# A gated-linear-attention and Mamba kernel: eleven warming matmuls of 64 columns in place of three of 256

## The chip, the cores and the metric

The kernel runs on one core of a Trainium2 chip. The time is the device time of one execution in microseconds, as the median of several runs; lower is better. A profiled execution has a time of its own and a span, the stretch from the first to the last record of its trace.

## The reference

Two blocks follow one another, all in fp32. The first is a recurrent attention with a gate alpha for every step and channel (B = 4, H = 8, S = 768, D = 48); the second takes its output as x (4 x 768 x 384) through a gated Mamba-like layer with an inner width of 512.

```python
for t in range(S):                                   # attention
    state = alpha[:, :, t, :, None] * state + einsum('bhd,bhe->bhde', k[:, :, t], v[:, :, t])
    y[:, :, t] = einsum('bhd,bhde->bhe', q[:, :, t], state)
x = y.transpose(0, 2, 1, 3).reshape(B, S, H * D)
val, gate = split(x @ w_in)                          # 384 x 1024
a = exp(A_log)
for t in range(S):                                   # one decay, a[0, 0], for all channels
    h = a[0, 0] * h + val[:, t, :]
    ys[:, t, :] = h
out = (silu(gate) * ys) @ w_out                      # 512 x 384
```

## The kernel before

The work is cut into twelve groups of 256 steps (three to a batch). In a group the alphas of 128 step-rows are brought into a layout with channels on partitions, scanned into cumulative products (`scan_P`, L635, and their inverse form `scan_V`, L654, on VectorE), and q and k are scaled by them. TensorE then makes the scores of the group's chunks (`scores`, L798), the values inside a chunk (`first_values`, L918, in the first group, `values`, L834, later), the states (`states`, L866) and what is carried from chunk to chunk (`first_carried`, L926, and `carried`, L847). `project` multiplies x by w_in (L988), scans h on VectorE (L995), applies the gate (L1006, L1008), and `output` multiplies by w_out (L1064).

The order of all instructions is written out by hand: the program is one long straight list per engine (a manual schedule), so an instruction's place in its engine's program is the order of the calls in the source. There are no loops left on the chip. At the end a flag is read and the program branches: in the usual case into a short block that makes the last outputs (twelve passes at L1377).

The head of the program, in order:

- Loads. `load_steps` (L422) brings alphas, q and k of the first groups on the queues of SP and ACT; `load_w` (L454) brings pieces of w_in as raw bits (`wbits`), two DMAs of 384 KB for each of the four pieces. On SP's queue at the head: alphas, q, k, alphas and k of the second group, the first two `wbits`, then q of the second group.
- `constants()` on GpSimd and others, which makes the identity `ident`.
- `keep_warm(3, 256)`: matmuls of a constant zero block by constant zeros, into the PSUM bank y0, which nothing reads before it is written anew. It depends on no load.
- `first_alphas` (L716 to L743): 64 turns of 64 x 64 on TensorE at L723, as soon as the first alphas have landed, and their copies out of PSUM. "Turn" means a matmul with the identity that transposes a tile.
- `first_q` (L745): turns of the first q at L750 and L759. `straighten(0, "k")`: turns of the first k at L702 and L703, and then those of the second alphas (`alphas(1)`) at the same lines.
- `scan_P(0)`, `scan_V(0)`, scaling, `scores(0)` (L798), with turns of the second k in two halves (`turned`, L702 and L703) ahead of and behind it.
- The first piece of w_in is put together from its bits (`low`, `high`, `add_low`, L543 to L556), then the second `load_w` is issued on SP, behind a one-element memset of its tile on VectorE (L1143).
- `first_values` (L918), `states(0)` (L866), a first half of the turns of the second q; then SP issues the alphas of the third group, the third `load_w`, and further loads.
- `first_carried` (L926), `first_values` again, the second half of the turns of the second q (L707), `first_join`, and from then on the projections (L988) with the work of the next groups between them.

Every fp32 matmul of a real product is two passes in the records: each pass has a weight load (LDWEIGHTS, engine PEld) and a MATMUL (engine PE).

Of the kernel before, what the change touches and what calls it, by code (L numbers as in the profile page):

```python
# [346 lines left out]
def fast(  # L347
# [339 lines left out]
    def bank(tag=None):  # L687
        if tag:
            return ps_at.tile([C, 512], FP32, tag=tag, name=tag)
        return ps_mm.tile([C, 512], FP32, tag=f"mm{next(taken)}", name="mm")  # L690
# [25 lines left out]
    def first_alphas():  # L716
        raw, to = steps_of("a", 0), by_runs(by_place(als[0])[:, :, 1:GP])
        tps = [[bank(tag)[:, 0:NJ // 2 * 64].rearrange("p (j x) -> p j x", x=64) for tag in tags]
               for tags in (("s0", "s1"), ("y1", "y0"))]

        def turn_quarter(j, i, r):
            rows = ds(64 * r, 64)
            nc.tensor.matmul(tps[j // 4][r][ds(64 * i, 64), j % 4], raw[rows, ds(i * ROW + j * D, 64)],  # L723
                             ident[rows, rows], start=True, stop=True, skip_group_check=True)

        for j in range(2):
            for r in range(2):
                turn_quarter(j, 1, r)
        for j in range(NJ):
            for r in range(2):  # L730
                turn_quarter(j, 0, r)
                if j + 2 < NJ:
                    turn_quarter(j + 2, 1, 1 - r)
        copies = []
        for n in range(2):
            for r in range(2):
                place = to[:, :, ds(16 * r, 16), 4 * n:4 * n + 4]
                part = tps[n][r].rearrange("p j (c h) -> p h c j", h=4)
                copy = nc.vector.tensor_copy(out=place, in_=part) if r else \
                    nc.scalar.activation(place, part, AF.Copy)  # L740
                for other in copies[1 - r::2]:
                    tc.declare_no_dep(copy.ins, other.ins, reason="the copies write different steps")
                copies.append(copy)  # L743
# [32 lines left out]
    def keep_warm(n, w):  # L776
        t = bank("y0")
        for _ in range(n):
            nc.tensor.matmul(t[:, 0:w], nc.const_aps.tensor(0.0, [C, C], FP32),
                             nc.const_aps.tensor(0.0, [C, w], FP32), start=True, stop=True,  # L780
                             skip_group_check=True)
# [334 lines left out]
        for _ in range(count):  # L1116
            next(steps, None)

    keep_warm(3, 256)
    first_alphas()  # L1120
    for t in sums:
        nc.scalar.activation(t[:, :, D:64], wide_S[0][:, 0:4 * (64 - D)].rearrange("p (j d) -> p j d", j=4), AF.Copy)
# [234 lines left out]
@with_exitstack  # L1357
def kernel(ctx: ExitStack, tc: tile.TileContext, *args):
    nc = tc.nc
    out = args[-1]  # L1360
    C, GC, NI = 128, 256, 4
    B, S, DM = out.shape
    keep = ctx.enter_context(tc.tile_pool(name="keep", bufs=1))
    ps_mm = ctx.enter_context(tc.tile_pool(name="ps_mm", bufs=1, space=bass.MemoryType.PSUM))
    w_outs = [keep.tile([C, 2, DM], FP32, name=f"w_out{i}") for i in range(2)]
    f_last = keep.tile([C, NI, GC], FP32, name="f_last")
    rows = ctx.enter_context(tc.tile_pool(name="rows", bufs=3))
    with tc.manual_schedule():
        good = fast(tc, *args, w_outs, f_last, ps_mm, rows)
    with tc.If(good <= 0, preferred_fallthrough_block=True, label="last") as choice:  # L1370
        general(tc, *args, w_outs)
    with choice.Else(), tc.manual_schedule():
        half = DM // 2
        for i, c, at, size in ((0, 0, 0, DM), (1, 1, 0, half), (3, 1, half, half)):
            o = ps_mm.tile([C, 512], FP32, tag=f"mm{i}", name="mm")[:, 0:size]
            for cc in range(NI):
                nc.tensor.matmul(o, f_last[:, cc, ds(c * C, C)], w_outs[cc // 2][:, cc % 2, ds(at, size)],  # L1377
                                 start=(cc == 0), stop=(cc == NI - 1))
            if not at:
                o_sb = rows.tile([C, DM], FP32, tag="o_sb", name="o_sb")  # L1380
            if c and not at:
                nc.vector.tensor_copy(out=o_sb[:, 0:half], in_=o)
            else:
                nc.scalar.activation(o_sb[:, ds(at, size)], o, AF.Copy)
            nc.scalar.dma_start(out=out[B - 1, ds(S - GC + c * C, C), ds(at, size)], in_=o_sb[:, ds(at, size)])
# [30 lines left out]
```

## Time and profile before

| | |
|---|---|
| median of 3 runs | 270.24 us |
| lowest and highest | 270.16, 270.4 us |
| the profiled execution, its own time | 270.68 us |
| its span | 269.0 us |
| busy of TensorE, VectorE, GpSimd, ScalarE | 98%, 87%, 61%, 41% of the span |
| granted TensorE clock | 1.0 |

Times in rows are in microseconds from the start of the span. In a timeline a row is a run of like instructions of one engine: start, duration up to the last result, engine, line, operation, tiles, shapes and count, and in brackets the idle time ahead of it with what ended it. In a row of windows the stretch comes first, then its length, and for each engine the busy time with the count of instructions that started in it; behind POOL stand the granted clock, the busy share of the 16 DMA engines and GB/s. A group row ends in busy time, mean duration of one in ns, and idle time before. In the list of DMA queues a row is the queue and kind, packets, MB, and the share of the time of 16 engines in the stretch asked for. A row of DMA issues ends in the size and the microseconds from issue to landing. "issue" as the cause of idle time means that the engine waited for nothing that the profile shows.

### The profile page before, as it was taken

How to read it: one execution, taken by the hardware profiler on the slowest of the kernel's cores; microseconds unless marked ns; L12 is line 12 of the kernel's file. 1: busy time of each engine (PE TensorE's matmuls, PEld its weight loads, DVE VectorE, ACT ScalarE, POOL GpSimd, SP SyncE). 2: the span in 40 equal slices, each digit the busy share in tenths (PEclk: the TensorE clock that was granted, in tenths of full speed). 3: DMA queues.
4: the chain of work that ended last, by engine and by line, in shares of the span. 5: the costliest groups of instructions: out<-in, count | busy, mean ns of one | idle time of the engine just before them, and what ended most of it. 6: DMA issues, size and time to landing. Idle time of an engine off the chain costs nothing.

```text
span 269.0 us, 9976 instructions
## 1 busy us (share of the span) xinstructions
PE 263.0 (98%) x4168; PEld 230.2 (86%) x4168; DVE 233.5 (87%) x316; ACT 111.6 (41%) x270; POOL 165.3 (61%) x185
## 2 busy tenths in 40 slices
PE   7989999999999999999999999999999999999995
PEld 5978889886688988988988988988988989988974
DVE  7978898996999999999999999999999998883440
ACT  4666776281242631632543533524524515314011
POOL 8222304093267998996985995996886987646000
PEclk9999999999999999999999999999999999999999
DMA  5938974796993659559687478569588501201201
GB/s 173 316 117 281 296 172 139 210 225 159 243 220 90 138 159 231 119 140 229 133 227 170 107 207 184 113 173 219 128 210 172 144 3 29 75 3 37 70 7 59
DMA packets 52304, 41.19 MB, mean 153 GB/s; under 512 B 27392, under 2 KB 50944, under 8 KB 52256
## 3 DMA queue, kind: packets, MB, share of 16 engines
q1 hardware_dynamic: 49328, 37.34, 56.1%
q0 software_dynamic: 1536, 2.20, 3.1%
q10 hardware_dynamic: 1392, 0.99, 1.3%
q8 instruction: 34, 0.56, 0.9%
q14 instruction: 14, 0.11, 0.1%
HBM read 32.54 MB, written 4.72 MB: 139 GB/s over the span
## 4 chain that ended last, share of the span: by engine, by line
PE 96%; DMA 2%; issue 0%; ACTq 0%; ACT 0%
PE mm L988 48%; PE mm L1064 16%; PE y L834 4%; PE y L847 4%; PE mm L1022 4%; PE s L798 4%; PE mm L798 3%; PE s L866 3%; PE mm L707 2%; PE mm L1377 2%; DMA raw_q<-in_q_dram 2%; PE mm L702 2%; PE mm L703 1%; PE y L918 1%; PE mm L750 1%; PE y L926 1%
## 5 line engine op out<-in xcount | busy, mean ns | idle before, releaser
L988 PE MATMUL mm<-xT,w_in 128*128 128x256 f32 x576 | 129.4, 382 | 0.0
L988 PEld LDWEIGHTS mm<-xT,w_in 128*128 128x128 f32 x576 | 107.9, 190 | 16.0 <-issue 0.5
L1006 ACT ACTIVATE sg<-mm 128x256 f32<-128x256 f32 x48 | 18.4, 383 | 88.9 <-PE mm L988 88.9
L1008 POOL TENSOR_TENSOR f_last<-sg,hh 128x256 f32<-128x256 f32 x36 | 28.8, 806 | 26.1 <-ACT sg L1006 22.6
L886 POOL TENSOR_TENSOR sum<-sum,dS 128x192 f32<-128x192 f32 x30 | 39.3, 1310 | 3.0 <-ACT dS L874 1.4
L635 DVE TENSOR_TENSOR_SCAN P<-al,lower 128x1028 f32<-128x1028 f32 x12 | 30.5, 2541 | 0.3
L995 DVE TENSOR_TENSOR_SCAN hh<-a_dec,hh,mm 128x256 f32<-128x256 f32 x32 | 23.3, 728 | 8.4 <-PE mm L988 8.2
L654 DVE TENSOR_TENSOR_SCAN V<-al,ends 128x1028 f32<-128x1028 f32 x12 | 28.5, 2375 | 0.4
L963 POOL DMA_DIRECT2D xT<-yst x44 | 22.6, 518 | 5.4 <-ACT yst L960 4.0
L556 POOL TENSOR_TENSOR w_in<-w_in,wr 128x768 int32<-128x768 int32 x4 | 7.3, 1820 | 26.3 <-DVE wbits L1143 9.3
L1064 PE MATMUL mm<-wide,wr 128*128 128x192 f32 x108 | 20.8, 327 | 0.0
L600 DVE STREAM_TRANSPOSE k<-raw_k 128x1024 f32<-128x1024 f32 x9 | 18.5, 2053 | 0.0
L600 DVE STREAM_TRANSPOSE q<-raw_q 128x1024 f32<-128x1024 f32 x9 | 18.2, 2026 | 0.0
L1064 PEld LDWEIGHTS mm<-wide,wr 128*128 128x128 f32 x108 | 18.0, 190 | 0.0
L874 ACT ACTIVATE dS<-s 128x384 f32<-128x384 f32 (+1 forms) x18 | 7.4, 461 | 24.4 <-PE s L866 24.4
L818 POOL TENSOR_TENSOR AK<-AK,mask 128x512 f32<-128x512 f32 x9 | 13.7, 1520 | 5.9 <-ACT AK L814 5.7
L600 DVE STREAM_TRANSPOSE al<-raw_a 128x1024 f32<-128x1024 f32 x8 | 16.4, 2045 | 0.0
L619 DVE TENSOR_TENSOR Zk<-k,V 128x1024 f32<-128x1024 f32 (+1 forms) x14 | 15.8, 1128 | 0.1
L1064 PE MATMUL mm<-w_out,f_last 128*128 128x192 f32 x72 | 15.6, 339 | 0.0
L610 DVE TENSOR_TENSOR Zq<-q,P 128x1024 f32<-128x1024 f32 (+1 forms) x14 | 15.2, 1083 | 0.0
L847 PEld LDWEIGHTS y<-Zq,sum 48*64 48x64 f32 x656 | 11.6, 134 | 3.5 <-issue 3.0
L834 PE MATMUL y<-AK,v 64*64 64x64 f32 x352 | 14.5, 221 | 0.0
(188 smaller groups left out, 503.7 us busy)
## 6 DMA issues: line engine op xcount, KB each, us to landing
v<-in_v_dram SPq DMA_DIRECT2D x22, 192.0 KB, 3.6
out_dram<-o_sb SPq DMA_DIRECT2D x22, 192.0 KB, 2.7
raw_k<-in_k_dram SPq DMA_DIRECT2D x18, 184.0 KB, 4.6
raw_q<-in_q_dram SPq DMA_DIRECT2D x18, 184.0 KB, 4.7
raw_k<-in_k_dram SPq DMA_DIRECT2D x18, 176.0 KB, 4.9
raw_q<-in_q_dram SPq DMA_DIRECT2D x18, 176.0 KB, 4.7
wbits<-in_moe_w_in_dram SPq DMA_DIRECT2D x8, 384.0 KB, 5.7
raw_a<-in_alpha_dram SPq DMA_DIRECT2D x16, 184.0 KB, 3.6
```

The costliest lines, as they stand in the source:

```text
L600: nc.vector.transpose(out=by_runs(to).rearrange("p h c j -> p h j c"), in_=raws[name][:, 0:4 * ROW].rearrange("p (h j d) -> p h j d", h=4, ...
L635: nc.vector.tensor_tensor_scan(out=P, data0=al[:, 0:4 * GP], data1=lower.rearrange("p h t -> p (h t)"), initial=0.0, op0=ALU.mult, op1=ALU ...
L654: nc.vector.tensor_tensor_scan(out=V[:, ::-1], data0=al[:, 1:4 * GP + 1][:, ::-1], data1=ends.rearrange("p h t -> p (h t)")[:, ::-1], init ...
L798: nc.tensor.matmul(scs[m][c][i][ds(L * h, L), ds(p * (L + D), L + D)], Zk[rows, c, p, ds(h * L, L)], Zq[rows, u, p], start=True, stop=True ...
L834: nc.tensor.matmul(ys[m][i][ds(64 * s, 64), e, ds(c * C + h * L, L)], v_sb[rows, c, 4 * i + p, :], As[i][rows, c, p, :], start=across and ...
L847: nc.tensor.matmul(ys[m][i][ds(64 * s, 64), e, ds(u * L, L)], Ss[j][rows, p, :], Zqs[m % 2][rows, u, p, D:], start=False, stop=True, skip_ ...
L886: nc.gpsimd.tensor_add(Ss[j][:, :, 0:D], Ss[j - 1][:, :, 0:D], part)
L963: engines[n % len(engines)].dma_start(out=xT[to, a], in_=st[rows, i, e])
L988: nc.tensor.matmul((pv, pg)[vg], w_ins[cc][:, kk, vg, :], xT[:, kk, :], start=(kk == 0), stop=(kk == NK - 1))
L995: nc.vector.tensor_tensor_scan(out=hh, data0=a_dec[:, cc:cc + 1].to_broadcast([C, GC]), data1=pv, initial=prev_h[cc][:, GC - 1:GC] if n % ...
L1008: f = lambda: engine.tensor_mul(fs[n][cc], sg, hh)
L1064: nc.tensor.matmul(o, a[:, k], b[k] if type(b) is list else b[:, k], start=start and k == 0, stop=k == KC - 1, skip_group_check=True)
```

## The change

The warming matmuls at the head become eleven of 64 columns instead of three of 256. They stand in the same place, write the same bank and read the same constants. All else in the source is the same; on the other engines the instructions and their order are the same too. On TensorE, 22 passes stand ahead of the first turn where there were six.

```diff
-    keep_warm(3, 256)
+    keep_warm(11, 64)
     first_alphas()
```

with, unchanged,

```python
def keep_warm(n, w):
    t = bank("y0")
    for _ in range(n):
        nc.tensor.matmul(t[:, 0:w], nc.const_aps.tensor(0.0, [C, C], FP32),
                         nc.const_aps.tensor(0.0, [C, w], FP32), start=True, stop=True,
                         skip_group_check=True)
```

## The prediction

> **What bounds the kernel now.** I read the page first: busy shares, then the chain that ended last.
>
> ```profile
> PE 263.0 (98%) x4168; PEld 230.2 (86%) x4168; DVE 233.5 (87%) x316; ACT 111.6 (41%) x270; POOL 165.3 (61%) x185
> q8 instruction: 34, 0.56, 0.9%
> PE 96%; DMA 2%; issue 0%; ACTq 0%; ACT 0%
> L988 PE MATMUL mm<-xT,w_in 128*128 128x256 f32 x576 | 129.4, 382 | 0.0
> ```
>
> TensorE is busy 98% of the span and is 96% of the chain, so a delay or gain of TensorE that no later wait absorbs is carried to the end. The waits of PE over the whole span say where it is ever late:
>
> ```profile
> PE y L779 <- PEq L1400: 1.0, 1, 1.0
> PE y L926 <- issue: 0.8, 1, 0.8
> PE mm L750 <- DMA raw_q<-in_q_dram: 0.7, 1, 0.7
> ```
>
> Only three: the start, the first turned q at 6.29 us, and 0.8 us at L926 for which no semaphore is named ("issue"). The timeline of PE and PEld, with the group row of the six loads, shows the places:
>
> ```profile
> 1.00 2.92 PE L779 MATMUL y<-const-float32-0.0 128*128 128x256 f32 x6 [1.00 <-PEq L1400]
> 0.99 2.21 PEld L779 LDWEIGHTS y<-const-float32-0.0 128*128 128x128 f32 x6 [0.99 <-issue]
> L779 PEld LDWEIGHTS y<-const-float32-0.0 128*128 128x128 f32 x6 | 1.8, 328 | 1.3 <-issue 1.0
> 4.03 0.88 PE L723 MATMUL s<-ident,raw_a 64*64 64x64 f32 x25
> 6.29 1.96 PE L750 MATMUL mm<-ident,raw_q 128*64 128x128 f32 x24 [0.71 <-DMA raw_q<-in_q_dram]
> 8.18 0.63 PE L759 MATMUL mm<-ident,raw_q 128*64 128x128 f32 x4
> 18.86 0.46 PE L926 MATMUL y<-Zq,wide_S 48*64 48x64 f32 x16
> 20.16 0.39 PE L926 MATMUL y<-Zq,wide_S 48*64 48x64 f32 x7 [0.84 <-issue]
> 22.40 1.09 PE L707 MATMUL mm<-ident,raw_q 128*64 128x128 f32 x16
> 23.43 1.78 PE L988 MATMUL mm<-xT,w_in 128*128 128x256 f32 x7
> 25.40 0.73 PEld L988 LDWEIGHTS mm<-xT,w_in 128*128 128x128 f32 x4 [0.38 <-ACT a_dec L1167]
> ```
>
> L926 stops in the middle of 23 like passes, after its sixteenth, and goes on 0.84 us after the last result: not a missing operand, I read, but missing program. The page's q8 row holds 34 instruction packets with 0.56 MB, 16 KB each, for 2 x 4168 passes and loads, so one packet holds about 245 to 256 instructions, some 125 passes. Counts of passes up to each break (windows from the start) agree:
>
> ```profile
> 0.00:8.15 8.15, 6.32 (x94) 5.00 (x94) 6.46 (x23) 3.24 (x11) 6.87 (x16) 1.00 0.68 202
> 0.00:16.10 16.10, 14.27 (x219) 12.36 (x220) 13.47 (x34) 9.04 (x24) 6.87 (x16) 1.00 0.74 221
> 0.00:20.10 20.10, 17.49 (x346) 15.23 (x347) 16.51 (x40) 11.49 (x28) 8.70 (x17) 1.00 0.66 201
> 0.00:25.30 25.30, 22.63 (x474) 19.69 (x474) 21.50 (x46) 14.29 (x35) 8.70 (x17) 1.00 0.70 214
> ```
>
> PE's breaks at L926 (pass 346) and at L988's load (pass 474, where the load is 0.38 late) are 128 passes apart; 127 earlier lies pass 219, a small hitch at 16.1. So the program's blocks begin at passes 94, 219, 346 and 474. The DMA view of four narrow windows holds one q8 packet each: 13.7 to 15.0, 17.3 to 18.7, 22.8 to 23.9 us (in this order; the first had none between 4 and 13.5):
>
> ```profile
> q8 instruction: 1, 0.02, 5.5%
> q8 instruction: 1, 0.02, 5.8%
> q8 instruction: 1, 0.02, 5.0%
> ```
>
> Shares are of 16 engines: 0.055 x 16 x 1.3 = 1.14 us, 1.30 us and 0.88 us, so each nearly fills its window and the starts are 13.8, 17.35 and 22.9 us. The passes that each releases start at 16.1, 20.16 and 25.40: a block is usable 2.3 to 2.8 us after its fetch starts. After pass 474 PE has no gap in the waits above.
>
> **The change part by part.** *Count and columns.* Three fp32 matmuls are six passes (x6), so eleven are 22: 16 passes, 32 instructions, more. Columns fall from 6 x 256 to 22 x 64 per pass, 1536 to 1408. Six passes of 256 took 2.92 us to the last result, 0.43 us a step (2.92 less a tail of some 0.35, by six), 1.67 ns a column: 64 columns would stream in 0.107 us. The weight load of each is still 128 columns, and no row shows a load longer than its stream. Bounds for a step: 0.107 us (load wholly hidden; 22 steps, end near 3.6 us) and, from the 328 ns of one load record, which holds some latency too, an estimate of 0.21 us, the double (end near 5.7 us). The first turn waits until 4.03, by its PEld on the arrival of raw_a; the next DMA wait of PE ends at 6.29 with 0.71 us of idle. I take 0.107 to 0.17 us, end 3.6 to 4.9, because the six loads from 0.99 to 3.20 never delayed their streams. Cost: nothing; the cover is those 0.71 us. If the step is 0.21, the turns start 1.7 us late, PE's own idle absorbs 0.7, and what the Vector work behind the turns loses could cost up to 0.7.
>
> *The shift.* Every block boundary now falls 16 passes earlier in the code: old passes 78, 203, 330, 458 in place of 94, 219, 346, 474. Their times in the trace:
>
> ```profile
> 0.00:7.00 7.00, 5.17 (x78) 3.99 (x80) 5.31 (x23) 3.17 (x10) 5.78 (x15) 1.00 0.62 179
> 0.00:14.86 14.86, 13.03 (x202) 11.32 (x202) 12.57 (x31) 7.89 (x20) 6.87 (x16) 1.00 0.79 238
> 0.00:18.85 18.85, 17.02 (x330) 14.86 (x330) 15.26 (x39) 10.81 (x26) 8.38 (x17) 1.00 0.66 199
> 0.00:22.85 22.85, 20.18 (x458) 17.85 (x460) 19.16 (x43) 11.89 (x30) 8.70 (x17) 1.00 0.69 208
> ```
>
> Block by block, with the loads that share the DMA engines (issue rows of SP, and landing times of single issues at 7.73, 17.63 and 20.26 us):
>
> ```profile
> 6.84 1.26 SPq L454 DMA_DIRECT2D wbits<-in_moe_w_in_dram  x2
> 8.15 1.36 SPq L422 DMA_DIRECT2D raw_q<-in_q_dram  x2
> 17.21 1.80 SPq L454 DMA_DIRECT2D wbits<-in_moe_w_in_dram  x2
> 19.67 1.19 SPq L422 DMA_DIRECT2D raw_a<-in_alpha_dram  x2
> wbits<-in_moe_w_in_dram SPq DMA_DIRECT2D x1, 384.0 KB, 8.2
> wbits<-in_moe_w_in_dram SPq DMA_DIRECT2D x1, 384.0 KB, 4.5
> raw_a<-in_alpha_dram SPq DMA_DIRECT2D x1, 192.0 KB, 5.1
> ```
>
> A fetch is asked for, as I read it, when PE enters the block before: 8.15 for the one that starts at 13.8, 16.1 for 17.35 (1.2 us, with little else to move), 20.16 for 22.9, where the two wbits loads and the first raw_a were queued ahead.
>
> First block, needed at 14.86 instead of 16.1: asked for at 7.0 instead of 8.15, so between the two wbits issues and no longer behind both. It needs to start by 12.4; the second wbits lands at 7.73 + 8.2 = 15.9, its fetch went 2.1 us ahead of that, and with only one of the two ahead it should be 2 to 3 us earlier, 10.8 to 11.8. Expected stall 0, and the hitch at 16.1 (0.1) goes.
>
> Second block, needed at 18.86: asked for at 14.86, start up to 14.9 + 1.2 = 16.1, or 16.4 if the raw_q loads of 8.15 hold it; usable at 18.4 to 19.2. Stall 0 to 0.3 in place of 0.84 at L926: PE runs 0.7 to 1.0 us ahead of before from there, 0.95 by the value that I take, no stall and the hitch of 16.1 gone too.
>
> Third block, needed now at pass 458, in the L707 turns. Without the old stalls PE would be there near 21.9 (22.85 less 0.95). It is asked for near 18.9 and ready to start by 20.1 at the latest: behind the wbits issue of 17.63 that takes 4.5 us to land (22.1), and before or among the raw_a packets. By the first block's relation the fetch goes 1.1 to 2.1 us ahead of that landing: 20.0 to 21.0. I take 21.0, the late end, since the third fetch of before also went only at 22.9, after all of it. Usable at 23.3 to 23.8: a stall of 1.4 to 1.9 in the L707 turns. From pass 458 to 474 lie half of the sixteen L707 passes, 0.55 us, and eight of L988 at 129.4 / 576 = 0.225, 1.80: 2.35 us. Pass 474 started at 25.40 before. With the middle of 2.3 to 2.8, and a little for the restart, 2.65 from start to use, it starts later by (start + 2.65 + 2.35) - 25.4 = start - 20.4. For 21.0: **+0.6 us**, and 0 at 20.4. Bounds: -0.4 (20.0) to +1.0 (21.4).
>
> Later blocks had no stall; a pass takes 263.0 / 4168 = 0.063 us in the mean, so 125 of them 7.9 us, against some 4 us (1.2 + 2.7) that a fetch needs. Blocks of short passes lie between, so I cost the shift there at nothing, at most 0.3 us. At the end the program branches and fetches its last blocks:
>
> ```profile
> 260.28 3.39 PE L1377 MATMUL mm<-w_out,f_last 128*128 128x384 f32 x12
> ```
>
> L988 passes run up to 260.28 without a gap and hide the branch; the boundary there moves onto the first L1377 load, whose fetch starts some 2.7 us ahead of use: 0, with +2.7 if it were asked for only at the branch.
>
> Sum on the profiled execution: 270.68 + 0.6 = 271.3. It lies 0.44 above the median of 270.24, so the median goes to 270.8.
>
> **The rivals.** *1, the other side: the third fetch does not wait for the wbits queue.* If it starts as soon as asked for, 18.9 to 20.1, PE keeps most of the 1 us: start - 20.4 = -1.5 to -0.3, -1.0 at 19.4. POOL's add of the next w_in limits it to some -1.1, since it runs to 27.15 and L988 needs it near 28.4:
>
> ```profile
> 25.34 1.81 POOL L556 TENSOR_TENSOR w_in<-w_in,wr 128x768 int32<-128x768 int32 x1 [6.17 <-ACT q L714]
> ```
>
> It gives 270.24 - 1.0 = 269.2. It decides where the start is before 20.4. For it: the second fetch started after 1.2 us; against it: the first and third took 5.6 and 2.7 us under queued loads. [...]
>
> *2: the fetch comes later than reckoned.* If the first fetch still waits for both wbits loads it starts at 13.8 again, is usable at 16.1 and costs 1.3 at pass 203; the later two then start when they did, 17.35 and 22.9, with 16 passes more behind them: 22.9 - 20.4 = +2.5. If instead the third waits behind the first raw_a, about 21.6 to 22.9, it is +1.2 to +2.5. Together 271.4 to 272.7, middle 272.1.
>
> *3: nothing moves.* If the gap at L926 isn't missing program, 16 passes ahead of a covered wait change nothing: 270.2. [...]
>
> [...]
>
> **How the numbers follow.** Forecast (third fetch behind wbits, +0.6) 0.42; rival 1 0.29; rival 2 0.16; rival 3 0.06; rival 4 0.07. A measurement of this kernel can tell 0.2%, 0.54 us. Faster by more: nearly all of rival 1 and the lowest of the forecast, 0.29. Within: 0.16 of the forecast's 0.42 (its -0.4 to +0.5), rival 3, a little of the rest, 0.23. Slower: 0.48. The time is 270.8; the forecast's own range is 269.9 to 271.3. The range for 8 in 10 reaches to rival 1's limit, 269.1, and to the middle of rival 2 with some more, 272.3.
>
> **What would show it.** Right: 22 L779 passes ending by about 4.0; L926 at 18.9 without a gap; a gap "issue" of 1.4 to 1.9 us inside L707 near 22 us, before any L988; one q8 packet starting about 21.0; the last L988 of the project that starts at 23.43 later by 0.6. Rival 1: that packet before 20 and no gap over 0.5 at L707. Rival 2: a gap at 14.9, or the packet after 21.6. Wrong altogether: the gap still after sixteen L926 passes, or first turns later than 4.5 us.

## The result and the profile after

The change is slower: 273.6 us (273.13 to 273.83, four runs) against 270.2 (269.88 to 270.4, four runs), a ratio of 1.013 with a 95% interval of 1.0114 to 1.0146, or +3.4 us. The forecast was 270.8, its range ended at 272.3. The profiled execution after took 273.83 us with a span of 272.1.

The page of after: TensorE is still the bound, and busy for 3.9 us more.

```profile
PE 266.9 (98%) x4184; PEld 235.1 (86%) x4184; DVE 233.8 (86%) x316; ACT 111.7 (41%) x270; POOL 164.9 (61%) x185
PE 98%; issue 0%; ACT 0%
```

Its waits of PE, the rows that answer to the three shown of before:

```profile
PE y L779 <- PEq L1400: 1.0, 1, 1.0
PE mm L707 <- issue: 0.9, 1, 0.9
```

The gap in L926 is gone, one in L707 has come, and the wait for the first q is gone because PE now comes later than q. The timeline of PE after, at the head and around that gap:

```profile
1.00 4.94 PE L779 MATMUL y<-const-float32-0.0 128*128 128x64 f32 x22 [1.00 <-PEq L1400]
5.87 1.19 PE L723 MATMUL s<-ident,raw_a 64*64 64x64 f32 x30
8.05 3.35 PE L750 MATMUL mm<-ident,raw_q 128*64 128x128 f32 x24
11.33 0.63 PE L759 MATMUL mm<-ident,raw_q 128*64 128x128 f32 x4
21.79 0.62 PE L926 MATMUL y<-Zq,wide_S 48*64 48x64 f32 x22
24.27 0.66 PE L707 MATMUL mm<-ident,raw_q 128*64 128x128 f32 x8
25.79 0.66 PE L707 MATMUL mm<-ident,raw_q 128*64 128x128 f32 x8 [0.86 <-issue]
26.38 2.86 PE L988 MATMUL mm<-xT,w_in 128*128 128x256 f32 x12
```

Three things are to be read here. The 22 warm passes end at 5.94, so a step is about 0.21 us (4.94 less the tail of the last, by 22; from the second pass on their starts are 213 ns apart), and the first turn starts at 5.87 instead of 4.03. The 24 passes of L750 take 3.35 us instead of 1.96: they run at half speed, with starts 213 ns apart (8.32, 8.53, 8.74) where those of before are 109 apart (6.45, 6.56, 6.67). Up to 10.6 us a pass lasts 426 ns in the mean, in before 277; the turns at L702 that follow last 273 in both. In before the turns of L723 go from 366 ns to 217 by 4.31. I call this speeding up the rise of the clock: near 10.9 us after, near 4.3 before, and the low clock is the stretch ahead of it. (The column of granted clock shows 1.0 over both stretches, as the first two rows below have it; the slow start is seen only in the durations.) So L759 starts at 11.33 instead of 8.18, 3.15 us late. And L707 breaks after eight of its sixteen passes, which is old pass 458, the boundary that the shift by 16 puts there: in the third row below, 474 passes have started ahead of the break, 458 and the 16 added.

```profile
8.00:10.80 2.80, 2.80 (x23) 2.75 (x22) 2.54 (x2) 1.27 (x7) 0.07 (x1) 1.00 0.99 297
10.80:14.00 3.20, 3.20 (x31) 3.03 (x29) 2.67 (x3) 2.06 (x4) 0.00 (x0) 1.00 0.96 299
0.00:25.75 25.75, 23.93 (x474) 22.53 (x475) 19.11 (x43) 12.63 (x33) 8.67 (x17) 1.00 0.60 188
```

Against the first trace of before, PE is 3.15 us late behind L750, 2.9 at the first L926, 1.9 behind its sixteenth pass (the old gap is saved), 2.9 behind the new gap in L707, and 3.16 at the last L1377.

### The profile page after: what moved, and what is told of

The parts are those of the page before. It is cut to its first block, busy times and chain, and to the rows that moved or that the text cites. A ratio compares the mean times of both kernels' runs of the same rounds, so it can differ in the third digit from the quotient of the medians.

```text
span 272.1 us, 10008 instructions
## 1 busy us (share of the span) xinstructions
PE 266.9 (98%) x4184; PEld 235.1 (86%) x4184; DVE 233.8 (86%) x316; ACT 111.7 (41%) x270; POOL 164.9 (61%) x185
## 4 chain that ended last, share of the span: by engine, by line
PE 98%; issue 0%; ACT 0%
PE mm L988 47%; PE mm L1064 16%; PE y L834 4%; PE y L847 4%; PE mm L1022 4%; PE s L798 4%; PE mm L798 3%; PE s L866 3%; PE mm L707 2%; PE mm L1377 2%; PE y L779 2%; PE mm L702 2%; PE mm L703 1%; PE mm L750 1%; PE y L918 1%; PE y L926 1%
## 5 line engine op out<-in xcount | busy, mean ns | idle before, releaser
L988 PE MATMUL mm<-xT,w_in 128*128 128x256 f32 x576 | 129.2, 382 | 0.0
L988 PEld LDWEIGHTS mm<-xT,w_in 128*128 128x128 f32 x576 | 108.0, 190 | 15.6 <-issue 0.5
L995 DVE TENSOR_TENSOR_SCAN hh<-a_dec,hh,mm 128x256 f32<-128x256 f32 x32 | 23.3, 728 | 8.3 <-PE mm L988 8.1
L834 PE MATMUL y<-A,v 64*64 64x64 f32 x352 | 14.7, 221 | 0.0
```

Source lines behind the costliest of these rows:

```text
L834: nc.tensor.matmul(ys[m][i][ds(64 * s, 64), e, ds(c * C + h * L, L)], v_sb[rows, c, 4 * i + p, :], As[i][rows, c, p, :], start=across and ...
L988: nc.tensor.matmul((pv, pg)[vg], w_ins[cc][:, kk, vg, :], xT[:, kk, :], start=(kk == 0), stop=(kk == NK - 1))
L995: nc.vector.tensor_tensor_scan(out=hh, data0=a_dec[:, cc:cc + 1].to_broadcast([C, GC]), data1=pv, initial=prev_h[cc][:, GC - 1:GC] if n % ...
```

## The experiments

In all of them but e11 and e12, which run the change and before as they are, `keep_warm` was given one or two more arguments, the weight columns `p` and, where needed, the bank `t`; nothing that the outputs depend on is left out in any of them. A "short" matmul is one weight column by one streamed column: two passes of program in about 0.06 us (the 16 short passes of e5 begin at 5.98 and L750 follows them at 6.45, about 29 ns a pass). Differences are of medians, in us, against runs of before on the same chip; before spread from 269.4 to 272.1 over these chips in nearly all of its runs, so under 0.3% only intervals count.

**The shift alone, at the head** (e1).

```diff
     keep_warm(3, 256)
+    keep_warm(8, 1, 1)
```

> The three warming matmuls of 256 columns stay, and eight more of one weight column and one streamed column follow them: 16 passes of program more, almost no time. Theory A (the 3.4 us come from the time of the warm passes and a later rise of the clock; the shift of the program only moves a gap): first turn near 4.0 us, turns as short as before, no gap inside L926, a gap of 0.8 to 1.9 us in L707; time 269.9 to 270.9. Theory B (the shift of the program is what costs): 272.5 or more, with PE late behind new gaps.

Measured 272.03, ratio 1.005 (1.0028 to 1.0073), times from 270.72 to 273.43. It misses Theory A's number and stays under B's. The profile tells why it is no clean test: the short passes made the first turn 0.4 us late, and the clock rose near 10.3 us, behind all of L750 (3.67 us for its 24 passes, 1.96 in before). Timeline of PE:

```profile
6.62 3.67 PE L750 MATMUL mm<-ident,raw_q 128*64 128x128 f32 x24
24.75 0.66 PE L707 MATMUL mm<-ident,raw_q 128*64 128x128 f32 x8 [0.82 <-issue]
```

**Shorter weight loads** (e2, and once more as e15), the change with 64 weight columns:

```diff
-    keep_warm(3, 256)
+    keep_warm(11, 64, 64)
```

> Eleven matmuls of 64 streamed columns, but with 64 weight columns instead of 128; 22 passes as in the change. Theory A1 (a load and its stream add up in these passes, 107 and 107 ns): steps of 160 ns, last warm result near 4.8 us, first turn near 4.7; time 270.5 to 273. Theory A2 (the load alone sets the step at 213 ns, hidden stream): steps of 107 ns, warm end near 3.6, clock up near 4.3, time as with the shift alone, 269.9 to 270.9. Theory B (shift): 272.5 or more with either step.

Measured 271.71, ratio 1.0055 (1.0036 to 1.0075). Timeline of PE of e2:

```profile
1.00 2.60 PE L779 MATMUL y<-const-float32-0.0 128*64 128x64 f32 x22 [1.00 <-PEq L1400]
3.90 1.16 PE L723 MATMUL s<-ident,raw_a 64*64 64x64 f32 x26 [0.30 <-DMA raw_a<-in_alpha_dram]
6.26 1.96 PE L750 MATMUL mm<-ident,raw_q 128*64 128x128 f32 x24 [0.28 <-DMA raw_q<-in_q_dram]
22.64 0.66 PE L707 MATMUL mm<-ident,raw_q 128*64 128x128 f32 x8 [0.56 <-issue]
```

As many passes, as much streamed, half the weight columns: 22 passes in 2.60 us, steps of 0.107, turns on time, L750 at full speed. The step is Theory A2's: it halves with the weight columns, 213 ns with 128 and 107 with 64, so the load sets it. The gap in L707 stays. The profiled execution took 270.40, but the median is 1.35 over before; A's number is missed again.

**Less to stream per load** (e4) and **fewer passes of 64 columns** (e3):

```diff
-    keep_warm(3, 256)
+    keep_warm(11, 16)      # e4
+    keep_warm(3, 64)       # e3
```

> Eleven matmuls of 16 streamed columns with 128 weight columns. Theory A1 (load and stream add): steps of about 134 ns, warm end near 4.1 us. Theory A2 (the load alone is 213 ns): steps of 213 ns as with 64 columns, first turn near 5.9. Either way the streams are sparse, and the clock should rise late; time 271.5 to 273.6.

> Three matmuls of 64 columns: program as long as before, warm passes end near 2.5 us, so the first turn is not late. Theory A (a clock that rises only after dense streaming): turns and L750 at half speed, first rise later than 7 us, time 271.0 to 272.5. Theory B (shift alone costs): as before, 270.2, within 0.5.

e4 took 274.29 (one run, above the 273.6 expected), e3 271.27, ratio 1.0029 (1.0012 to 1.0045). The rows of e4, then of e3:

```profile
1.00 4.87 PE L779 MATMUL y<-const-float32-0.0 128*128 128x16 f32 x22 [1.00 <-PEq L1400]
```

```profile
1.00 1.53 PE L779 MATMUL y<-const-float32-0.0 128*128 128x64 f32 x6 [1.00 <-PEq L1400]
6.21 3.58 PE L750 MATMUL mm<-ident,raw_q 128*64 128x128 f32 x24
```

A quarter of the columns, the same 0.21 us a step (4.87 us for 22 passes, 4.94 in the change): A2 again, what is streamed adds nothing to the step of 213 ns. In e3, with the program as long as before and no turn late, the poor warming alone keeps L750 at half speed (rise near 9.5 us) and costs 0.9.

**The shift alone, behind the first turns** (e5), **and lateness with and without it** (e7, e8).

```diff
     keep_warm(3, 256)
     first_alphas()
     ...
+    spare_bank = ps_mm.tile([C, 512], FP32, tag="mm3", name="mm")
+    keep_warm(3, 512, C, spare_bank)         # e7, e8 only; there keep_warm(3, 256) goes
+    keep_warm(8, 1, 1, spare_bank)           # e5, e8 only
     tq = first_q()
```

> The three warming matmuls of 256 columns stay; the eight with one weight and one streamed column now come behind the first turns, into the wait for the first q. So every block boundary from the second on lies 16 passes earlier, and the head is as before. Theory C (the shift moves the gap from L926 to L707 and is worth -0.4 us when PE is on time, as in the trace with 64 weight columns): no gap in L926, 0.6 to 0.9 us in L707, 269.8 to 270.4 against before. Theory D (the shift costs by itself, since the later gap is not covered by a late head): 0.8 to 1.5 us over before.

> No warm pass ahead of the first turns; three matmuls of 512 columns (six passes, so no shift) stand between the turns and L750, which makes PE about 3 us late at L750. Theory C (the gap in L926 takes up lateness when the blocks lie as before): PE 2.5 to 4 us late at L759, the gap in L926 gone, 1.2 to 2 us late at pass 474 and so 271.4 to 272.3. Theory D' (lateness of the head is carried whole): 273 or more.

> As the one before, with the eight short matmuls behind the 512-column ones: late by the same, and the boundaries 16 passes earlier. Theory C: the gap in L707 comes whatever the lateness, so it is 0.8 to 1.4 us slower than the one before. Theory D': the same as the one before within 0.5.

e5: 271.1, ratio 1.0046 (1.0028 to 1.0063), +1.1: Theory D. e7: 273.03, 1.0111 (1.0082 to 1.0141), +3.0, with L750 at 9.88, 3.6 late against 6.29: Theory D', the lateness is carried. It is not carried quite whole: against the profile of before it falls from 3.6 at L759 to 2.3 at the end of the span, since e7 has no gap in L926, and against that of e12 below from 4.1 to 3.1. e8: 275.16, 1.0181 (1.0149 to 1.0212), with L750 at 10.73: 0.85 later than in e7, and 2.1 slower, so some 1.3 is the shift's. That misses D' (the same as e7 within 0.5) and fits the part of Theory C by which the gap in L707 comes whatever the lateness. The other part, a gap at L926 that belongs to the kernel and brings the time of e7 down to 272.3, fell. The rows of e5, and of e8, at the gap:

```profile
23.07 0.66 PE L707 MATMUL mm<-ident,raw_q 128*64 128x128 f32 x8 [0.83 <-issue]
```

```profile
27.08 0.66 PE L707 MATMUL mm<-ident,raw_q 128*64 128x128 f32 x8 [0.86 <-issue]
```

**Before once more** (e12) showed where Theory C was wrong.

> The kernel before once more, for a second profile. [...] Theory F': at 4.3 again.

269.81 us (one run). The clock rose near 4.4, close to the 4.3 of Theory F'. L926 and L707 in its timeline, and then all its waits of PE:

```profile
18.87 0.62 PE L926 MATMUL y<-Zq,wide_S 48*64 48x64 f32 x22
21.35 1.09 PE L707 MATMUL mm<-ident,raw_q 128*64 128x128 f32 x16
```

```profile
PE y L779 <- PEq L1400: 1.0, 1, 1.0
PE s L723 <- DMA raw_a<-in_alpha_dram: 0.3, 1, 0.3
PE s L798 <- DVE Zq L610: 0.3, 1, 0.3
PE mm L798 <- ACT k L714: 0.2, 1, 0.2
```

There is no gap for missing program at all. Its DMA view has a q8 packet in the window from 8.8 to 10.1 us:

```profile
q8 instruction: 1, 0.02, 4.6%
```

The first fetch started near 9 us here, at 13.8 in the trace that the prediction used. The gap in L926 that I took for the kernel's own stands in one of two profiles of before. A late first fetch goes with it there, but does not make it alone: e3 and e7, unshifted too, have their first packet at 12.7 and 14.0 us and no gap in L926, with PE itself 1.3 and 3.4 us later there. Measured against the trace of e12, the shift costs 0.7 us in e2 and 1.0 in e15, the two profiles with 64 weight columns: the start of the ninth L707 pass, 22.64 and 22.75 against 21.84, less the lateness just ahead of it, 0.1 and -0.1.

**Smaller shifts** (e9 four short matmuls, e10 two, at e5's place).

> As the shift behind the first turns, with four short matmuls instead of eight: boundaries 8 passes earlier, at old passes 86, 211, 338 and 466. Theory C: the first block is still fetched early, the gap at L926 is gone, and the one at pass 466 is 0.5 us shorter than at 458, so 0.4 to 0.9 us faster than before in an execution whose clock rises by 6 us; lateness of the head is carried on where the clock rises later. Theory D (the shift costs by itself): as with 16 passes or slower, 0.5 to 1.5 us over before.

> Two short matmuls, 4 passes, boundaries at 90, 215, 342 and 470. Theory C: if the first fetch is early enough (start by 12 us), no gap over 0.3 us anywhere and 0.8 to 1.2 us faster; if it still starts behind the queued wbits loads near 13.8, the gap in L926 is there as before, and the time is that of before within 0.5.

e9: 270.5, ratio 1.0015 (0.9997 to 1.0034); e10: 270.44, 1.0011 (0.9994 to 1.0027). Neither can be told from before. The rows: e9's gap, at pass 466, the first of L988, as the boundaries say, and e10's waits of PE, with none for program.

```profile
22.83 2.86 PE L988 MATMUL mm<-xT,w_in 128*128 128x256 f32 x12 [0.37 <-issue]
```

```profile
PE y L779 <- PEq L1402: 1.0, 1, 1.0
PE s L723 <- DMA raw_a<-in_alpha_dram: 0.3, 1, 0.3
```

So the gap moves with the boundary and shrinks as more of the longer L707 and L988 passes come ahead of it: 0.83 at 458 (e5), 0.37 at 466, none at 470, or at 474 in e12. The gain that I expected of both, and that did not come, was a gain over the accidental gap.

**The change once more** (e11), **and with dense streams** (e6, once more as e14: `keep_warm(11, 128)`).

> The change itself, once more, for its spread and a second profile. [...] Theory F' (the rise is fixed by the program): rise again at 10.9 us, spread under 0.8.

> Eleven matmuls of 128 columns: as many passes and weight loads as in the change, streams twice as long, dense. Theory E (the weight load of 213 ns sets the step while the clock is low, and sparse streams keep the clock low): steps of 213 ns to the rise, which now comes by 4.3 to 6.5 us; warm end near 5.0 to 5.7, L750 at full speed; faster than the change, 271 to 272.5. [...]

e11: 273.27 (273.19 to 273.64), ratio 1.0119 (1.0099 to 1.0139), +2.85; rise near 10.4, the gap in L707 at 0.8. The rise lies half a microsecond from F''s 10.9; the narrow spread, 0.45, speaks for F', a late rise in every run. e6: 273.08, +3.05, ratio 1.014 (1.0096 to 1.0184), above Theory E's 272.5, but its four times lay between 271.82 and 275.47, and the fastest is the one that was profiled; so it was run again beside e15 and a longer warming, e13 (`keep_warm(4, 256)`).

> Eleven matmuls of 128 columns once more. Theory E (dense streams bring the early rise): rise by 7 us, median 1.0 to 1.8 us over before, clearly below the change's 2.9 to 3.4. [...]

> Eleven matmuls of 64 columns with 64 weight columns once more: turns on time, dense, boundaries as in the change. Theory I (the moved boundary alone costs the gap in L707, 0.6 to 1.0 us, against executions of before that have no gap): median 0.7 to 1.5 us over before, gap in L707 again, none in L926. Theory C (shift worth -0.4 on time): median at or below before.

> Four matmuls of 256 columns: two passes more than before, dense until 4.4 us. Theory H (a longer dense stretch makes the early rise sure; the late end of 0.4 us is covered by the wait for the first q; boundaries 2 passes earlier, no gap of over 0.3 us): rise by 4.6 us, 0.1 to 0.5 us faster than before and a narrower spread. Rival: the first turns 0.4 us late cost that, 0.2 to 0.5 us slower.

e14: 272.08, ratio 1.0081 (1.0056 to 1.0106), +1.9. e15: 271.42, 1.0045 (1.0026 to 1.0065), +1.2. e13: 271.0, 1.0022 (0.9999 to 1.0045), +0.8: not told from before and no gain; its first turn is at 4.70, and its clock rose near 5.4, not by 4.6. Timeline of PE of e14:

```profile
1.00 4.76 PE L779 MATMUL y<-const-float32-0.0 128*128 128x128 f32 x22 [1.00 <-PEq L1400]
6.94 1.96 PE L750 MATMUL mm<-ident,raw_q 128*64 128x128 f32 x24
24.61 0.66 PE L707 MATMUL mm<-ident,raw_q 128*64 128x128 f32 x8 [1.38 <-issue]
```

Twice the streamed columns of the change, the same count of passes and loads, and it is faster, since L750 is at full speed, 1.96 us (rise near 5.3 us, in e6 near 6.3). That is Theory E; e14's median is a little over its upper bound of 1.8, and its profile has a long gap in L707, 1.38. From the first turn to L759 the profiles of e14 and e6 take 3.1 and 3.3 us, those of the change and e11 5.5 and 5.2.

The three kernels with 22 warm passes and the same boundaries put the 3.4 us together:

| | over before | what it adds |
|---|---|---|
| 64 weight and 64 streamed columns (e2, e15) | +1.35, +1.2 | the moved boundary |
| 128 weight and 128 streamed columns (e14; e6) | +1.9; +3.05 | steps of 213 ns, first turn near 5.7 |
| 128 weight and 64 streamed columns (the change, e11) | +3.4, +2.85 | clock up near 10.5 instead of 5 to 6 |

By e14, with eleven runs, that is about 1.2, 0.6, and 1.0 to 1.5. By e6, with four, the second step would take nearly all of the rest, so the medians don't fix the split between the last two; the profiles show both, and what made e6's slower executions slow was not traced.

## Why the prediction was wrong

**Columns and count, costed at nothing: the step that failed.** I named both ends of the step, 0.107 and 0.21, and took 0.107 to 0.17 for the reason that six loads "never delayed their streams". Those streams lasted 0.43 us, twice the 213 ns at which the loads follow one another after the change, so they could not have shown it. The step was 213 ns, the end that I had set aside; the turns came 1.84 us late, at 5.87, past the 4.5 that I had set as the sign of being wrong. The cover named, 0.71 us of wait for q, took its part, and the rest went through. (The wait of PEld ahead of the first turn, which I put down to raw_a, is put down by the trace that I read to a copy on GpSimd, Zq at L517; e2 and e12 name raw_a.)

**The clock was in no term of the sum.** I counted columns and the end of the warm stretch, not the share of time in which something streams: 107 ns in each 213, an estimate from 64 columns at the 1.67 ns a column of the six passes of before. In six profiles with warm streams of 256 columns and the turns next behind them (before near 4.3, e12 near 4.4, e10, e9, e13 and e5 from 4.6 to 5.6), and in e2, e15, e6 and e14 (4.5 to 6.3), the rise came by 6.3 us; with sparse ones (the change twice, e4, and e3, where they are also few) between 8.8 and 10.9. In e7 and e8, with no warm pass ahead of the turns, it came near 7.9 and 8.8, earlier than in the change. The late rise cost L750 alone 3.35 - 1.96 = 1.4 us. Rival 4, a step of 0.21 us and a later clock, had both at +0.5 to +2.7 and a chance of 0.07; both came, the chance was set low, and the measured +3.4 lies above that price. No run had shown by how much later the clock would rise; the runs showed it near 10.9 and 10.4 us in the change against 4.3 and 4.4 in before. That dense streams alone decide was not settled: e1, dense for 2.6 us and then short passes, rose near 10.3.

Counted from the first pass, the early rises came after 3.3 to 5.3 us, those of e7 and e8 after 4.0 and 4.8, those with sparse streams after 7.8 to 9.9. By what rule the clock rises was not shown.

**The shift: right place, wrong baseline.** L926 ran through and L707 broke after eight passes, as written. The boundary that I set at pass 94, by the pause ahead of L759, is none: that pause stays ahead of L759 with 16 passes more in front. Those at 346 and 474 are borne out. The DMA view after, windows from 10.1, 18.1 and 23.2 us:

```profile
q8 instruction: 1, 0.02, 5.6%
q8 instruction: 1, 0.02, 5.4%
q8 instruction: 1, 0.02, 5.0%
```

The first fetch came early, as expected; the third started near 23.3, 1.5 us after the first L926 pass, with which its block ahead begins. The gap was 0.86, not 1.4 to 1.9. Counted from the same pass of the trace that I read (18.86), that start is 20.4, where my formula gives 0, and not 21.0 with +0.6: the wait behind the `wbits` loads that I put in was too long, and the packet came at the border to rival 1, which asked for one before 20 and no gap over 0.5.

The gap needs no such wait. In eight of the ten profiles shifted by 16 passes the third packet starts 1.4 to 1.6 us after the first pass of the block ahead (2.0 and 2.1 in e14 and e4), the first pass that it brings starts 2.3 to 2.6 us later, and the 128 passes in between are done in 3.0 us (e12, 18.87 to 21.84).

Rival 2's late first fetch had already happened, in the trace of before that I read. I set the gain of 0.84 us at L926 against the new gap; of the two profiles of before only that one has a gap to give. So the term was +1.1 to +1.35 by the medians of e5, e15 and e2, instead of +0.6. Their profiles show 0.7 to 1.0 of it against e12; they are among the fastest executions of their kernels, and the rest was not traced. Rival 3 fell: the gap followed the boundary over shifts of 8 and 16 passes. Most blocks of this kernel were crossed without a wait: the page counts 34 instruction packets, and the waits of PE put at most one gap in a profile down to "issue", in those shifted by 8 or 16 passes this one, which cost 0.4 to 1.4 us.

**The end of the program** and the later blocks: PE's lateness went from 2.9 behind L707 to 3.16 at the end, 0.3, the bound that I gave. No wait at the branch.

What stays open: why the first fetch of before starts at 9 us in one execution and at 13.8 in another, and whether the 1.4 to 1.6 us before the third are the loads' doing or the fetch's own. No order of the loads was tried for it.

## What to carry to other kernels

Price small matmuls by their weight load (here 213 ns a pass for 128 weight columns and 107 for 64, at the low clock), and don't take a load for hidden from a trace in which every stream is longer than it. For a warming stretch, count the share of its time in which columns stream: 64 columns to a step of 213 ns streamed half of the time, by the estimate above, the stretch grew longer, and the clock rose 4 to 6 us later than behind as many passes of 128 columns (10.9 and 10.4 against 5.3 and 6.3). And before a gap in one trace is entered as the kernel's own, look for it in a second execution.

## What the runs showed of the hardware

- At the low clock fp32 passes with 128 weight columns followed one another every 213 ns, whether they streamed 16, 64 or 128 columns (e4, the change, e14), and with 64 weight and 64 streamed columns every 107 ns (e2, e15).
- The instructions came in packets of 16 KB, 34 of them with 0.56 MB on the page, and breaks for missing program stood at fixed places of TensorE's program, passes 346 and 474 of before. A gap of 0.4 to 1.4 us of "issue" stood at the boundary behind a block of some 128 short passes that lasts only about 3 us (18.87 to 21.84 in e12), while 3.7 to 4.5 us passed from its first pass to the first of the next block's; adding 8 or 16 passes far ahead moved it by as many.
- The page's granted clock read 1.0 while the starts of L750's passes were 213 ns apart in the change and 109 in before.
